# Sliding-window attention and a mixture of experts: one value load split, some work reordered, fillers added

## The chip, the cores and the metric

The kernel runs on one core of a Trainium2 chip. A core has a matrix engine (PE in the profile), a vector engine (DVE), a scalar engine (ACT), a general engine (POOL) and a sync engine (SP) that here only issues transfers. Each engine works through its own queue in order, and engines wait for one another by semaphores. Sixteen DMA engines move data between main memory and on-chip memory; transfers issued by POOL and by SP go through queues of their own, q0 and q1 in the profile. Matrix products land in PSUM, a small accumulator memory that DVE and ACT read. The metric is the device time of one execution in microseconds (us).

## What is computed

Attention over 8 batches of 8 heads, 576 positions, head size 64, in which a position sees itself and the 63 before it; its output is the input of a mixture of experts with one expert per batch:

```python
scores = scale * np.matmul(q, k.transpose(0, 1, 3, 2))
mask = (rel >= 0) & (rel < window)                 # window = 64
attn = softmax(np.where(mask, scores, -1e9))
x = np.matmul(attn, v)        # heads side by side: [8, 576, 512]
e_idx = np.argmax(x.mean(axis=1) @ w_gate, axis=1) # one of 8 experts per batch
h = np.maximum(x[b] @ w1[e_idx[b]], 0.0)           # w1: [8, 512, 1024]
out[b] = gate_w[b] * (h @ w2[e_idx[b]])            # w2: [8, 1024, 512]
```

Only the chosen expert of a batch is loaded. Which one it is, is known only when that batch's whole attention is done.

## The kernel before

**Units.** The work on attention is cut into 16 units: unit `t` is half of the heads of batch `t // 2`. A unit's q and k (`load_qk`, on POOL's queue, cast to bf16 on the way) are transposed on PE (`transpose_qk`) and copied out of PSUM by ACT or DVE (`leave_qk`). Then come three groups of scores (`scores(t, c)`, c = 0, 1, 2): small matmuls, an exp on ACT (line 389), and a multiplication by a 0/1 mask on DVE (line 396, `mask_out`). Units 0 and 1 do without the multiplication: there `add_outside` puts large negative numbers into PSUM with two matmuls per group, before the scores are added.

**Values.** `values(t, s)` multiplies the probabilities by v (line 417) and normalises on DVE (lines 431 and 433). v of a batch comes as one fp32 transfer on SP's queue (`load_v`, 36 blocks of 64 columns for 128 partitions). `cast_part` makes two fp16 copies of a unit's half of it: the whole tile (`va`), and two shifted halves, `low` and `high` (`vb`). Three fp32 v buffers are used in turn. The transfer is held back by a one-element write of POOL into the tile, and that write may read something that has to be there first (`behind`).

**Gate and experts.** After a batch's second unit, `transpose_x` turns x round, ACT also sums it, DVE multiplies the sums with the gate's weights, `gate` picks the expert and POOL loads its number into a register; `load_w1` and `load_w2` then fetch the two weight matrices (1 MB each in fp16). `expert_up` (line 561, eight per batch) makes h with ReLU on ACT (line 565), `expert_down` (line 575, and line 584 for the last 64 positions) makes the output, which DVE or ACT copies into one of six `ob` buffers, and SP sends it off (lines 579 and 592), five copies per batch.

**The order** is written out by hand, and each engine keeps it (`P` is `tc.keep_in_program_order`). A prologue handles units 0 to 3 and batch 0's gate line by line. Then a loop over `t` from 4 on mixes a unit of attention with pieces of the experts of earlier batches: each `experts(pace)` call takes about one `expert_up` or `expert_down` from a stream. In even `t` the loop also runs `next_gate` for batch `t // 2 - 1`, which issues that batch's weights, v of batch `t // 2 + 2`, and q and k. Four PSUM buffers are shared by everything. `busy(n)` issues n matmuls of 128x512 on a constant tile; nothing reads what they give.

The lines the change touches: `load_v` at 219, `cast_part` at 305, `gate` at 490, `load_w1` at 530, `load_w2` at 542, `expert_up` at 549, `expert_down` at 567, the prologue, and the loop body.

Of the kernel before, what the change touches and what calls it, by code (L numbers as in the profile page):

```python
# [156 lines left out]
def kernel(  # L157
# [10 lines left out]
    nc = tc.nc  # L168
# [49 lines left out]

    def load_v(b, behind=None):
# [7 lines left out]
        P(nc.sync.dma_start(out=vn, in_=vv[b]))  # L227
        v_tiles[b] = vn

    HM = NM // 2  # L230
# [240 lines left out]
    w1c = moe_w1.rearrange("e (kb p) f -> e p kb f", p=128)  # L471
    w2e = moe_w2.rearrange("e (g p i) d -> e p g i d", p=128, i=4)

    gparts = {}
# [15 lines left out]
    def gate(b):  # L490
# [3 lines left out]

        glog = small.tile([128, E], FP32, tag="glog")
        P(nc.vector.tensor_copy(out=glog, in_=gl[:, 0, 0:E]))
        gmx = small.tile([128, 8], FP32, tag="gmx")
# [25 lines left out]

    NQ = 2

    def w1_parts():
        return weights[0][0].rearrange("p k f -> p (k f)").rearrange(
            "p (h k f) -> p h k f", h=NQ, k=KB)

    def load_w1(b):  # L530
        if b == 0:

            src = w1c[experts_of[b]].squeeze(0)
            for hf in range(NQ):
                P(nc.gpsimd.dma_start(out=w1_parts()[:, hf],
                                      in_=src[:, :, ts(hf, F // NQ)]))
# [12 lines left out]
    def expert_up(b, ft):  # L549
        if b == 0:  # L550
            w1t, cols = w1_parts()[:, ft // 4], slice(ft % 4, 512, 4)
        else:
            w1t, cols = weights[b][0], slice(512 * (ft // 4) + ft % 4, 512 * (ft // 4 + 1), 4)
# [15 lines left out]
    def expert_down(b, mt):  # L569
# [3 lines left out]
        if mt < 4:  # L573
            for fb in range(FB):
                P(nc.tensor.matmul(  # L575
                    out=pso[:, 0, :], lhsT=hT[:, fb, ts(mt, 128)],
                    rhs=w2t[:, fb, :], start=(fb == 0), stop=(fb == FB - 1)))
            copy_on(nc.scalar if mt == 1 else nc.vector, ob, pso[:, 0, :])
            P(nc.sync.dma_start(out=out[b, ts(mt, 128), :], in_=ob))
# [184 lines left out]
    for t in range(START + 1, NU + LAG):  # L764
# [3 lines left out]
        def next_gate():  # L768
# [106 lines left out]
```

## Time and profile before

| what | us |
|---|---|
| median of 3 runs | 226.37 (226.18 to 226.79) |
| profiled execution | 226.16 |
| its span, first to last instruction | 224.1 |
| PE busy | 201.5 |
| DVE busy | 129.5 |
| ACT busy | 134.2 |
| POOL busy | 37.9 |

The table's lower part is from the first part of the profile's page. The second part cuts the span into forty slices of 5.6 us. The timeline gives instructions of one engine in order, with the idle time before each and what ended it in brackets. The view of waits adds up such idle times by who waited for whom. The chain of work follows the last instruction back to what released it, step by step. The view of stretches gives the engines' busy time, the granted PE clock and the DMA engines' share for any stretch of time. Lines such as L561 are lines of the kernel file.

### The profile page before, as it was taken

What the parts mean: (1) busy time and instruction counts of PE and PEld (TensorE: products, weight loads), DVE (VectorE), ACT (ScalarE), POOL (GpSimd) and SP (SyncE); (2) the same over time, 40 slices, a digit from 0 to 9 for tenths busy, and PEclk for the clock granted to TensorE, in tenths of its full rate; (3) what the DMA queues carried; (4) which work ended last, traced back from release to release, by engine and by line L of the source; (5) the groups of instructions that cost most, each with busy time, mean ns of one, the idle gap of its engine ahead of it and who ended that gap; (6) DMA issues with size and microseconds to landing.
All of it is one profiled execution on the core that took longest, in us unless ns stands there. A gap on an engine that the chain in (4) does not pass through costs nothing.

```text
span 224.1 us, 6989 instructions
## 1 busy us (share of the span) xinstructions
PE 201.5 (90%) x3011; PEld 141.9 (63%) x3012; DVE 129.5 (58%) x310; ACT 134.2 (60%) x220; POOL 37.9 (17%) x67
## 2 busy tenths in 40 slices
PE   7569779998799999989999998999999998999970
PEld 2247757755487568865686656875787557659630
DVE  2449695576856969284755667395939472420130
ACT  2176785963669656873869374967496557416400
POOL 7080360061000700052001600050002000200000
PEclk9988799999999999999999999999999999999996
DMA  5999999999999999999999999989955991399132
GB/s 70 239 253 244 159 188 218 245 251 226 231 233 249 252 214 240 235 283 207 246 229 300 169 236 228 271 203 221 243 155 87 212 256 40 56 225 255 68 140 69
DMA packets 29910, 45.64 MB, mean 204 GB/s; under 512 B 2480, under 2 KB 21936, under 8 KB 29872
## 3 DMA queue, kind: packets, MB, share of 16 engines
q0 software_dynamic: 13840, 26.22, 65.2%
q1 hardware_dynamic: 15232, 18.88, 27.5%
q8 instruction: 25, 0.41, 0.7%
q10 hardware_dynamic: 800, 0.03, 0.2%
q14 instruction: 13, 0.11, 0.1%
HBM read 61.90 MB, written 9.44 MB: 318 GB/s over the span
## 4 chain that ended last, share of the span: by engine, by line
PE 61%; DMA 13%; DVE 11%; ACT 8%; issue 3%; POOL 1%; POOLq 0%
PE php L561 24%; PE pso L575 19%; DMA w1t<-in_moe_w_dram 8%; ACT xT L462 5%; PE tp L334 5%; DMA kn<-in_k_dram 4%; PE op L417 4%; PE pso L584 3%; ACT hT L565 2%; DVE pt L396 2%; PE sp L374 2%; DVE vb L303 2%; DVE x L433 2%; PE tp L454 2%; PE gl L492 1%
## 5 line engine op out<-in xcount | busy, mean ns | idle before, releaser
L561 PE MATMUL php<-xT,w1t 128*128 128x288 f16 x512 | 70.0, 287 | 2.1 <-DMA w1t<-in_moe_w_dram 2.1
L565 ACT ACTIVATE hT<-php,gatew 128x576 f16<-128x576 f32 x64 | 47.1, 743 | 28.7 <-PE php L561 28.6
L561 PEld LDWEIGHTS <-w1t 128*128 128x128 f16 x512 | 56.0, 115 | 8.6 <-DMA w1t<-in_moe_w_dram 2.4
L575 PE MATMUL pso<-w2t,hT 128*128 128x512 f16 x256 | 60.2, 380 | 0.0
L389 ACT ACTIVATE pt<-sp 128x768 f16<-128x768 f32 x48 | 36.3, 815 | 9.3 <-PE sp L374 9.3
L575 PEld LDWEIGHTS <-hT 128*128 128x128 f16 x256 | 23.1, 98 | 25.8 <-issue 1.2
L303 DVE COPY ob<-pso 128x512 f32<-128x512 f32 x24 | 16.5, 688 | 24.4 <-PE pso L575 24.3
L538 POOL DMA_DIRECT2D w1t<-in_moe_w_dram x7 | 5.1, 730 | 136.7 <-DVE pt L396 91.9
L433 DVE TENSOR_TENSOR x<-op,linv 128x640 f16<-128x640 f32 x32 | 26.4, 825 | 1.1
L347 ACT COPY dst<-tp 128x1152 bf16<-128x1152 bf16 x16 | 17.9, 1120 | 14.0 <-PE tp L334 13.7
L396 DVE TENSOR_TENSOR pt<-pt,masks 128x768 f16<-128x768 f16 x42 | 22.8, 555 | 4.6 <-ACT pt L389 3.4
L462 ACT ACTIVATE xT<-tp 128x576 f16<-128x576 f16 x28 | 17.9, 646 | 6.3 <-PE tp L454 6.2
L417 PE MATMUL op<-vb,pt 128*64 128x65 f16 x320 | 17.0, 196 | 2.9 <-DVE pt L396 2.1
L417 PEld LDWEIGHTS <-pt 128*64 128x64 f16 x640 | 14.2, 111 | 5.7 <-DVE pt L396 2.5
L417 PE MATMUL op<-va,pt 128*64 128x65 f16 x320 | 16.7, 196 | 0.0
L303 DVE COPY vb<-va 64x1152 f16<-64x1152 f16 (+1 forms) x32 | 16.1, 504 | 0.7
L374 PE MATMUL sp<-dst 64*64 64x128 bf16 (+1 forms) x672 | 14.3, 218 | 1.6 <-ACT dst L301 0.8
L374 PEld LDWEIGHTS <-dst 64*64 64x64 bf16 x672 | 10.3, 110 | 8.5 <-issue 4.9
L484 DVE SCALAR_TENSOR_TENSOR gpart<-wg,pooled,gpart 128x8 f32<-128x8 f32 x21 | 4.8, 227 | 18.5 <-ACT xT L462 18.4
L431 DVE RECIPROCAL linv<-op 128x10 f32<-128x10 f32 x32 | 6.9, 216 | 13.7 <-PE op L417 13.6
L334 PE MATMUL tp<-ident,kn 128*64 128x128 bf16 x288 | 11.3, 225 | 2.9 <-DMA kn<-in_k_dram 2.9
L303 DVE CAST va<-vn 128x1152 f16<-128x1152 f32 x16 | 12.1, 758 | 3.2 <-DMA vn<-in_v_dram 3.1
(71 smaller groups left out, 178.6 us busy)
## 6 DMA issues: line engine op xcount, KB each, us to landing
w2t<-in_moe_w_dram POOLq DMA_DIRECT2D x8, 1024.0 KB, 17.3
out_dram<-ob SPq DMA_DIRECT2D x32, 256.0 KB, 6.8
w1t<-in_moe_w_dram POOLq DMA_DIRECT2D x7, 1024.0 KB, 9.1
qn<-in_q_dram POOLq DMA_DIRECT2D x16, 288.0 KB, 11.8
kn<-in_k_dram POOLq DMA_DIRECT2D x16, 288.0 KB, 12.8
w1t<-in_moe_w_dram POOLq DMA_DIRECT2D x2, 512.0 KB, 6.5
out_dram<-ob SPq DMA_DIRECT2D x16, 64.0 KB, 6.8
vn<-in_v_dram SPq DMA_DIRECT2D x8, 0.2 KB, 19.5
```

The costliest lines, as they stand in the source:

```text
L303: P(eng.tensor_copy(out=out, in_=in_))
L334: P(nc.tensor.transpose(out=tp[64 * s:64 * s + 64, ts(t, 128)], in_=src[:, s, ts(t, D)], identity=ident, tile_position=(0, 64 * s)))
L347: P(nc.scalar.copy(out=dst.rearrange("p (x r t) -> p x r t", x=2, t=NT), in_=view))
L374: P(nc.tensor.matmul(out=sp[64 * half:64 * half + 64, s, 64 * (qblk - 6 * c):64 * (qblk - 6 * c) + n], lhsT=kT[64 * s:64 * s + 64, ts(kblk ...
L389: P(nc.scalar.activation(out=pt, in_=sp[:, :, 0:384], func=AF.Exp, scale=scale))
L396: P(nc.vector.tensor_tensor(out=pt, in0=pt, in1=masks[:, c].rearrange("p s g w -> p s (g w)"), op=ALU.mult))
L417: P(nc.tensor.matmul(out=op[64 * half:64 * half + 64, xx, 65 * jj:65 * jj + 65], lhsT=pt[:, s, 64 * (g % 6):64 * (g % 6) + 64], rhs=win, s ...
L433: P(nc.vector.tensor_tensor(out=x[:, :, h0 * D:(h0 + 2) * D].rearrange("p j (x c) -> p x j c", x=2), in0=view[:, :, :, 0:64], in1=li[:, :, ...
L462: P(nc.scalar.activation(out=xT[:, kb, :], in_=tp[:, kl, 0:S], func=AF.Copy, accum_out=pooled[:, b, kb:kb + 1]))
L561: P(nc.tensor.matmul(out=php[:, sc, 0:288], lhsT=w1t[:, kb, cols], rhs=xT[:, kb, ts(sc, 288)], start=(kb == 0), stop=(kb == KB - 1)))
L565: P(nc.scalar.activation(out=hT[:, ft].rearrange("p (sc s) -> p sc s", sc=2), in_=php[:, :, 0:288], func=AF.Relu, scale=gatew[:, b:b + 1]))
L575: P(nc.tensor.matmul(out=pso[:, 0, :], lhsT=hT[:, fb, ts(mt, 128)], rhs=w2t[:, fb, :], start=(fb == 0), stop=(fb == FB - 1)))
```

## The change

It does eight things:

1. v of batch 3 comes in two transfers: blocks 0 to 19 where the whole transfer was issued before; the other 16 in the first pass of the loop, after the issue of batch 1's w1 and w2. The second is held by a POOL copy that reads a word of that w1.
2. Batch 0's w1 comes in three transfers of 256, 256 and 512 columns instead of two of 512; batch 0's w2 is read in runs of two rows instead of four, to fit. v of batch 2, held until the first half of w1 was there, is now held until the second of the three parts is there.
3. Batch 0's gate reads the logits out of PSUM and not from a copy.
4. In the prologue, two of unit 1's three `add_outside` move ahead of the transposes of its k, with two fillers; unit 1's whole-tile cast goes to ACT.
5. Fillers: `busy(1)` becomes `busy(3)` after unit 2's k, and `busy(2)` stands before batch 0's gate.
6. In the loop, from unit 6 on, the shifted halves of the next unit's v are cast after the third group of scores and its mask, not before.
7. The last output tile (batch 7, mt = 3) leaves PSUM in two halves, one by DVE and one by ACT, and goes out in two transfers, on SP's and on ACT's queue.
8. In even passes the gate's weight is also computed ahead of those shifted halves.

```diff
+    def load_rest(b, part, behind):
+        vn = v_tiles[b]
+        P(nc.gpsimd.tensor_copy(out=vn[:, part, 0:1], in_=behind))
+        P(nc.sync.dma_start(out=vn[:, part:NM, :], in_=vv[b][:, part:NM, :]))
...
+        if b:
+            glog = small.tile([128, E], FP32, tag="glog")
+            P(nc.vector.tensor_copy(out=glog, in_=gl[:, 0, 0:E]))
+        else:
+            glog = gl[:, 0, 0:E]
...
-    NQ = 2
+    PARTS = ((0, 256), (256, 256), (512, 512))
...
+            for i, (lo, n) in enumerate(PARTS):
+                P(nc.gpsimd.dma_start(out=w1_part(i), in_=src[:, :, lo:lo + n]))
...
-            out=weights[b][1].rearrange("p (g i) d -> p g i d", i=4),
-            in_=w2e[experts_of[b]].squeeze(0)))
+            out=weights[b][1].rearrange("p (g i) d -> p g i d", i=4 if b else 2),
+            in_=(w2e if b else w2f)[experts_of[b]].squeeze(0)))
...
+            if b == B - 1 and mt == 3:
+                oc = opool.tile([128, Dm], FP32, tag="ob", name="oc")
+                P(nc.vector.tensor_copy(out=ob[:, 0:256], in_=pso[:, 0, 0:256]))
+                P(nc.scalar.copy(out=oc[:, 0:256], in_=pso[:, 0, 256:512]))
+                P(nc.sync.dma_start(out=out[b, ts(mt, 128), 0:256], in_=ob[:, 0:256]))
+                P(nc.scalar.dma_start(out=out[b, ts(mt, 128), 256:512], in_=oc[:, 0:256]))
+                return
...
     transpose_qk(1, 0)
+    add_outside(1, 0)
+    add_outside(1, 1)
+    busy(2)
     transpose_qk(1, 1, leave=False)
     leave_qk(1, 1, A)
     load_qk(3)
     load_qk(4)
     cast_v(0)
-    cast_v(1)
-    for c in range(3):
-        add_outside(1, c)
+    cast_part(1, "whole", A)
+    cast_part(1, "low")
+    cast_part(1, "high")
+    add_outside(1, 2)
...
-    busy(1)
+    busy(3)
     pool_mm(1)
     pool_parts()
+    busy(2)
     gate(0)
...
-    load_v(2, w1_parts()[:, 0, 0, 0:1])
+    load_v(2, w1_part(1)[:, 0, 0:1])
     load_qk(6)
-    load_v(3)
+    load_v(3, part=20)
...
             load_w2(b)
+            if t == START + 1:
+                load_rest(3, 20, weights[b][0][:, 0, 0:1])
             if t // 2 + 2 < B:
                 load_v(t // 2 + 2)
...
             if gated:
                 cast_part(t + 1, "whole")
-            cast_part(t + 1, "low")
-            cast_part(t + 1, "high")
         experts(pace)
         if on:
             scores(t, 2)
         if gated and on:
             gate_weight(t // 2 - 1)
+        if ahead and t > 5:
+            cast_part(t + 1, "low")
+            cast_part(t + 1, "high")
```

More of the change, by code (lines that the diff above doesn't have):

```diff
@@ L217, with load_v @@
     v_tiles = {}
-    def load_v(b, behind=None):
+    def load_v(b, behind=None, part=0):
         vn = vpool.tile([128, NM, D], FP32, tag="vn")
@@ L226, in load_v @@
             P(nc.gpsimd.tensor_copy(out=vn[:, 0, 0:1], in_=behind))
-        P(nc.sync.dma_start(out=vn, in_=vv[b]))
         v_tiles[b] = vn
+        if part:
+            P(nc.sync.dma_start(out=vn[:, 0:part, :], in_=vv[b][:, 0:part, :]))
+        else:
+            P(nc.sync.dma_start(out=vn, in_=vv[b]))
+    def load_rest(b, part, behind):
+        vn = v_tiles[b]
+        P(nc.gpsimd.tensor_copy(out=vn[:, part, 0:1], in_=behind))
+        P(nc.sync.dma_start(out=vn[:, part:NM, :], in_=vv[b][:, part:NM, :]))
     HM = NM // 2
@@ L472 @@
     w2e = moe_w2.rearrange("e (g p i) d -> e p g i d", p=128, i=4)
+    w2f = moe_w2.rearrange("e (g p i) d -> e p g i d", p=128, i=2)
     gparts = {}
@@ L493, in gate @@
                            start=True, stop=True))
-        glog = small.tile([128, E], FP32, tag="glog")
-        P(nc.vector.tensor_copy(out=glog, in_=gl[:, 0, 0:E]))
+        if b:
+            glog = small.tile([128, E], FP32, tag="glog")
+            P(nc.vector.tensor_copy(out=glog, in_=gl[:, 0, 0:E]))
+        else:
+            glog = gl[:, 0, 0:E]
         gmx = small.tile([128, 8], FP32, tag="gmx")
@@ L522, with w1_part @@
     experts_of = {}
-    NQ = 2
-    def w1_parts():
-        return weights[0][0].rearrange("p k f -> p (k f)").rearrange(
-            "p (h k f) -> p h k f", h=NQ, k=KB)
+    PARTS = ((0, 256), (256, 256), (512, 512))
+    def w1_part(i):
+        lo, n = PARTS[i]
+        return weights[0][0].rearrange("p k f -> p (k f)")[
+            :, KB * lo:KB * (lo + n)].rearrange("p (k f) -> p k f", k=KB)
     def load_w1(b):
@@ L533, in load_w1 @@
             src = w1c[experts_of[b]].squeeze(0)
-            for hf in range(NQ):
-                P(nc.gpsimd.dma_start(out=w1_parts()[:, hf],
-                                      in_=src[:, :, ts(hf, F // NQ)]))
+            for i, (lo, n) in enumerate(PARTS):
+                P(nc.gpsimd.dma_start(out=w1_part(i), in_=src[:, :, lo:lo + n]))
         else:
@@ L550, in expert_up @@
         if b == 0:
-            w1t, cols = w1_parts()[:, ft // 4], slice(ft % 4, 512, 4)
+            part = min(ft // 2, 2)
+            at = 256 * (ft // 2) - PARTS[part][0]
+            w1t, cols = w1_part(part), slice(at + ft % 2, at + 256, 2)
         else:
```

## The prediction

> **What bounds the kernel.** I read the page's busy shares and forty slices first, then TensorE's (PE's) idle times in order of time, then the stretches that end in those idle times, then the DMA queues there. From the page:
>
> ```profile
> span 224.1 us, 6989 instructions
> ...
> PE 201.5 (90%) x3011; PEld 141.9 (63%) x3012; DVE 129.5 (58%) x310; ACT 134.2 (60%) x220; POOL 37.9 (17%) x67
> ...
> DMA  5999999999999999999999999989955991399132
> ```
>
> PE is busy 90% of the span, and from the second slice on the DMA engines are full too, up to about 160 us. So two limits lie close together: what shortens PE's waits helps only as long as the data then come. PE's idle times, from the timeline of PE (start, duration, in brackets the idle time before and what ended it):
>
> ```profile
> 14.30 0.69 PE L334 MATMUL tp<-ident,kn 128*64 128x128 bf16 x18 [1.61 <-DMA kn<-in_k_dram]
> ...
> 22.83 0.28 PE L675 MATMUL pool<-once,x 128*128 128x1 f16 x5 [0.49 <-DVE x L433]
> 23.72 0.36 PE L492 MATMUL gl<-gpart,onesf 128*128 128x8 f32 x2 [0.61 <-DVE gpart L686]
> ```
> ```profile
> 50.79 0.19 PE L417 MATMUL op<-vb,pt 128*64 128x65 f16 x1 [0.40 <-DVE vb L303]
> ...
> 60.06 1.17 PE L561 MATMUL php<-xT,w1t 128*128 128x288 f16 x8 [1.63 <-DMA w1t<-in_moe_w_dram]
> ```
> ```profile
> PE op L417 <- DVE pt L396: 2.1, 4, 1.1
> ...
> PE op L417 <- DVE vb L303: 0.8, 2, 0.4
> ```
>
> The last fence is the view of PE's waits (total, times, longest): four waits, 2.1 us, before the values' matmuls are ended by a mask (pt L396), all after 61 us, and there little else is left for PE to win. Before it the largest wait is the 1.63 us for batch 1's w1, at 60.06. What an earlier stage saves counts only as far as it arrives there.
>
> **The change, part by part.** (1) *Fourth v in two transfers.* Batch 1's w1 is asked for late and lands later. In the chain of work (start, duration):
>
> ```profile
> 26.19 5.47 DMA w1t<-in_moe_w_dram
> ...
> 46.75 13.26 DMA w1t<-in_moe_w_dram
> ```
>
> The DMA queues (packets, MB, share of 16 engines) from 48 to 52 us, then from 52 to 60, then the landing time of the w1 issued at 192 us:
>
> ```profile
> q1 hardware_dynamic: 910, 0.92, 104.1%
> q0 software_dynamic: 52, 0.05, 7.7%
> ```
> ```profile
> q0 software_dynamic: 352, 1.38, 85.0%
> q1 hardware_dynamic: 429, 0.43, 22.2%
> ```
> ```profile
> DMA to landing us min/median/max: 7.9/7.9/7.9
> ```
>
> The last is w1 of batch 7, issued with nothing else in flight: 7.9 us, against 13.26 here. From 48 to 52 us the SP queue (q1, v in small packets) moves 0.92 MB and POOL's queue (q0, weights, q and k) 0.05, though w1 was issued at 46.75; from 52 to 60 q1 still moves 0.43 MB beside it. v of batch 3 is 4608 runs of 256 B, 1.18 MB; the change leaves 16 of 36 blocks, 0.52 MB, until w1 has landed. That is the 0.43 MB and 0.09 of the flood. Beside q1, q0 ran 1.38 MB in 8 us; without it I give it the rate of q0 alone under (2), 0.90 MB in 4.5 us, so w1's 1.05 MB take 5.2 instead of 6.1 us, and the flood (0.92 MB in 4 us) ends 0.4 us sooner: w1 lands at 58.7 instead of 60.0. Bounds: 60.0, if the order of q0 alone sets it; 46.75 + 7.9 = 54.7, if nothing is in the way. PE stands ready at 60.06 - 1.63 = 58.43. I take 60.06 - 58.7 = 1.4 us, since the row of 52 to 60 prices it nearest; ends 0 and, if PE is also ready sooner, 2.5.
>
> The Trainium skill, "DMA: Bandwidth & Descriptors", section "Queues, rings and completion order", says that each DMA engine takes turns between queue rows packet by packet. By that, q1's small packets would have taken turns with w1's large ones from 48 on; the two rows of 48 to 52 do not show it (52 packets against 910), the rows after 52 do (352 against 429). By the rule alone w1 would gain only the 0.9 us of its share, and the sum below would be 2.3 instead of 2.8 us.
>
> What waits instead: the rest of v is held on POOL by a copy that reads w1, so POOL stands until w1 lands, with v of batch 4 and q, k of units 7 and 8 behind it; SP stands too, with v of batch 4 and the first outputs behind. The rows are, in turn: the output issued between 52.1 and 52.3 us (the last number is its landing time), ACT's seventh copy of an output, the first php of batch 2, and the landing time of the w1 issued between 74.4 and 74.6.
>
> ```profile
> out_dram<-ob SPq DMA_DIRECT2D x1, 256.0 KB, 22.5
> ```
> ```profile
> 76.50 0.59 ACT L301 COPY ob<-pso 128x512 f32<-128x512 f32 x1 [0.72 <-PE pso L575]
> ```
> ```profile
> 84.10 1.14 PE L561 MATMUL php<-xT,w1t 128*128 128x288 f16 x8
> ```
> ```profile
> DMA to landing us min/median/max: 9.1/9.1/9.1
> ```
>
> q and k lie behind w2 in q0 anyway, so their later issue costs nothing. The first output lands at 52.2 + 22.5 = 74.7; there are six ob buffers, five outputs a batch, so the seventh copy (76.50, on ACT) needs it: 1.8 us of room. PE coming 1.4 us sooner uses most of it up. Batch 2's w1 lands at 74.5 + 9.1 = 83.6 and is used at 84.1: 0.5 us of room, with more of v and outputs now beside it. I charge 0.6 us for the two together, ends 0 and 2 (as much as w1 of batch 1 loses now).
>
> (2) *w1 of batch 0 in three, w2 in shorter runs.* One more issue on POOL. Packets become 512 and 2048 B. The two halves' issue on POOL, and q0 from 28.5 to 33 us, where it runs alone with w1's halves:
>
> ```profile
> 26.19 1.50 POOL L535 DMA_DIRECT2D w1t<-in_moe_w_dram  x2 [10.09 <-DVE gatew L520]
> ```
> ```profile
> q0 software_dynamic: 893, 0.90, 122.3%
> ```
>
> Packet time, q0: 122.3% of 16 engines in 4.5 us over 893 packets of about 1024 B is 0.099 us; 85.0% of 16 in 8 us over 352 of mostly 4096 B is 0.309. On that line a 512 B packet is 0.064. The first quarter (512 packets) then flows in 2.1 us, the old half in 3.2: it comes 1.1 us sooner (PE's wait there is 0.46, below), but the first half needs 4.1, 1.0 later, and w2 (2048 B, 0.17) 0.4 more. So q0 gets 1.4 us more work, beside a POOL issue of 1.50/2 = 0.75.
>
> (3) *Gate without its copy, casts of unit 1 shared, masks added early.* Timelines of DVE, ACT, PE, DVE again, and the landing time of the v issued between 31.9 and 32.1 us:
>
> ```profile
> 15.20 0.76 DVE L303 CAST va<-vn 128x1152 f16<-128x1152 f32 x1 [3.09 <-DMA vn<-in_v_dram]
> ...
> 17.76 0.92 DVE L303 COPY vb<-va 64x1152 f16<-64x1152 f16 x2
> ...
> 24.12 0.17 DVE L496 COPY glog<-gl 128x8 f32<-128x8 f32 x1 [0.54 <-PE gl L492]
> ```
> ```profile
> 15.04 1.12 ACT L301 COPY dst<-tp 128x1152 bf16<-128x1152 bf16 x1 [0.24 <-PE tp L334]
> 17.55 2.21 ACT L389 ACTIVATE pt<-sp 128x768 f16<-128x768 f32 x3 [1.39 <-PE sp L374]
> ```
> ```profile
> 31.71 0.56 PE L561 MATMUL php<-xT,w1t 128*128 128x288 f16 x3 [0.46 <-DMA w1t<-in_moe_w_dram]
> ```
> ```profile
> 49.45 0.79 DVE L303 CAST va<-vn 128x1152 f16<-128x1152 f32 x1
> ```
> ```profile
> DMA to landing us min/median/max: 17.4/17.4/17.4
> ```
>
> DVE casts without a break from 15.20 to 18.68, then norms follow back to back. With unit 1's whole tile on ACT behind the k copy (15.04 + 1.12 = 16.16; a copy of as many elements, so another 1.12) the two halves run 17.3 to 18.25: 0.45 us sooner. ACT's three exps start near 17.3 instead of 17.55, as four of six mask matmuls move into PE's 1.61 us wait. The gate drops 0.17 + 0.03 us. So w1 of batch 0 goes out 0.6 us sooner and PE is up to 1.1 us ahead at 31.71 (both 0.46 and the earlier scores). None of it passes 49.45: the cast of unit 4 starts as v of batch 2 lands (32.0 + 17.4 = 49.4), and PE waits for that cast at 50.79. That v starts behind the first half of w1, which comes 1.0 - 0.6 us later. I take 0 for all of this at 51 us (ends 0.9 us lost and 0.9 won).
>
> (4) *Fillers.* Six more 128x512 matmuls in the waits of 1.61, 0.49 and 0.61 us. They hold the clock. Stretches of 3.41 us, with each engine's busy time; the column before the last two is the granted clock:
>
> ```profile
> 11.57:14.98 3.41, 1.66 (x61) 1.27 (x52) 0.54 (x4) 3.23 (x4) 3.29 (x5) 1.00 1.11 242
> 14.98:18.39 3.41, 3.41 (x62) 1.99 (x62) 3.05 (x6) 1.96 (x3) 1.13 (x2) 0.50 1.13 254
> ...
> 21.80:25.22 3.42, 2.18 (x63) 1.66 (x60) 2.13 (x10) 1.85 (x3) 0.00 (x0) 1.00 1.20 219
> 25.22:28.63 3.41, 3.41 (x50) 3.21 (x48) 2.81 (x7) 3.12 (x8) 2.44 (x4) 0.50 0.65 98
> ...
> 49.11:52.52 3.41, 2.58 (x57) 1.86 (x55) 2.74 (x7) 1.70 (x2) 2.00 (x3) 1.00 1.12 226
> ```
>
> 0.50 follows a stretch with 1.66 of 3.41 us busy, and one with 2.18, much of it very small matmuls; it does not follow the last row, 2.58. Filled, both should stay at 1.00. A filler is about 0.22 us at full clock, 0.4 at half; two fit before the gate's matmul (0.61). Cost 0 (0.4 us if the clock is half, hidden by the v of batch 2), gain inside (3).
>
> (5) *Shifted halves behind the third mask.* DVE in unit 6:
>
> ```profile
> 75.04 1.16 DVE L303 COPY vb<-va 64x1152 f16<-64x1152 f16 x2
> ```
>
> The two halves (1.16 us) stand ahead of the mask. Moved, the mask is done about 1.1 us sooner, as much as the longest of the four waits; of that one I leave 0.2, because an output copy stays ahead of the mask. DVE's sum is unchanged, so what follows starts when it did. 1.9 us, ends 0 and 2.1.
>
> (6) *Last output in halves.* DVE and SP at the end:
>
> ```profile
> 217.38 0.69 DVE L303 COPY ob<-pso 128x512 f32<-128x512 f32 x1 [1.40 <-PE pso L575]
> ```
> ```profile
> 216.01 2.10 SPq L592 DMA_DIRECT2D out_dram<-ob  x2
> 218.19 0.54 SPq L579 DMA_DIRECT2D out_dram<-ob  x1
> ```
>
> The copy of 0.69 us falls to about 0.4, but SP is busy to 218.11 with the two outputs before; only the ACT half leaves at 217.9. I take 0.1 us, ends 0.3 won and 0.3 lost (a second queue to close).
>
> Sum: 1.4 + 1.9 + 0 + 0.1 - 0.6 = 2.8 us. The profiled execution took 226.16 us, 2.1 over its span, so 223.4; it is 0.2 below the median of 226.37, so I forecast a median of **223.6**. Its own range, 222.3 to 224.7, is by the ends of (1): 1.1 more won there, with up to 0.2 in (5), or 1.1 less. Under 0.3% (0.7 us) a measurement can't tell from no change.
>
> **The rivals.** *The queue was the limit* (0.22): q0 gets 1.4 us more, w1 of batch 1 still lands near 60, or its gain goes at batch 2's w1. For it: DMA full from slice 3; against: q1's 0.43 MB really are out of the way. Left are (5) and (6): 226.4 - 2.0 = 224.4, and 225.4 with another 1 us lost later.
>
> *The clock falls at 52.5* (0.10). If PE is 1.0 us ahead and v of batch 2 is not, the stretch 49.11 to 52.52 keeps 2.58 - 1.0 = 1.6 us busy, less than the 1.66 after which 0.50 followed. The next stretch is full, 3.42 us, and half a clock adds 1.7: PE is ready for w1 at 58.43 + 1.7 = 60.1, (1) is gone, and 224.5 is left. The Trainium skill, "TensorE: Matmul & The Clock Gate", section "Part 1: The HAM clock gate", has the rate halve only after an idle window of about 3.4 us. By that rule nothing of the kind would happen and 223.6 stands; the trace has shown 0.50 after half-busy windows, so I keep the rival.
>
> *Slower: outputs held on SP* (0.12). SP has nothing to move from about 51 us, when the first part of v is through, until w1 lands near 58.7: 7.5 us. If that isn't made up, the first output lands at 74.7 + d, with d up to 7.5, and ACT's copy, then wanted at 76.5 - 1.4 = 75.1, waits d - 0.4, with a PSUM buffer held. It decides from d = 4.5 on (3.4 won without the 0.6, plus 0.7); at d = 5.5 the time is 226.4 - 3.4 + 5.1 = 228.1. For it: DMA full everywhere; against: q0 runs faster meanwhile, so most of it is made up.
>
> The remaining 0.06 is for parts that cancel to within 0.3%. Forecast 0.50. Faster: 0.50 + 0.21 + 0.09 = 0.80; same 0.07; slower 0.13. The range 221.8 to 226.0 takes in both middle rivals and the gain at w1's far end, and leaves out the slower case.
>
> **What would show it.** Right: no idle before batch 1's first php (60.06), or under 0.4 us; no idle ended by pt L396 before 65-column matmuls; granted clock 1.00 from 5 us to the end; PE still waiting near 51 us for vb, and longer than 0.8. Wrong: w1 of batch 1 landing at 60 again, idle before php near 82, an output copy on ACT near 75 that waits for a DMA, or a 0.50 after 49.

## The result and the profile after

The changed kernel takes 229.86 us (median of 4 runs, 228.49 to 230.84) where the kernel before takes 226.58 beside it (226.18 to 226.87): a ratio of 1.0147, 95% interval 1.0117 to 1.0178, so 3.3 us slower. The forecast was 223.6, with 226.0 as the upper end: the sign is wrong. Ratios and intervals leave out the runs that took over 1.5% longer than the fastest of the same kernel, medians take in all runs, so for a kernel with two groups of times the two can differ.

The profiled execution took 229.3 us, 1.7 over its span. From its page:

```profile
span 227.6 us, 7012 instructions
...
PE 202.0 (89%) x3018; PEld 140.1 (62%) x3018; DVE 127.8 (56%) x308; ACT 135.0 (59%) x222; POOL 39.4 (17%) x69
...
PEclk9999999999999979999999999999999999999997
...
DMA packets 34310, 45.64 MB, mean 201 GB/s; under 512 B 7136, under 2 KB 26208, under 8 KB 34272
```

The prologue keeps its full clock (9 from the first slice on; before, slices 3 to 5 had 8, 8 and 7). A 7 now stands in slice 15, that is after 80 us, where there was none. And 7136 packets are smaller than 512 B, where the kernel before had 2480. PE's idle times, from its timeline, then what PE waited for between 40 and 120 us (total, times, longest):

```profile
50.99 0.19 PE L425 MATMUL op<-vb,pt 128*64 128x65 f16 x1 [1.25 <-DVE vb L311]
...
59.13 1.14 PE L577 MATMUL php<-xT,w1t 128*128 128x288 f16 x8 [0.66 <-DVE ob L311]
...
81.78 1.17 PE L342 MATMUL tp<-ident,qn 128*64 128x128 bf16 x18 [4.47 <-ACT ob L309]
```
```profile
PE tp L342 <- ACT ob L309: 4.5, 1, 4.5
PE op L425 <- DVE vb L311: 1.5, 2, 1.3
```

The php of batch 1 starts at 59.13 instead of 60.06, and no mask (now line 404) ends a wait any more. What is new is one wait of 4.47 us before the transposes of unit 7's q. PE waits there for ACT, whose copy of an output (line 309) stood for 6.33 us. ACT's row, then the chain of work (start, duration), then SP's queue:

```profile
81.15 0.59 ACT L309 COPY ob<-pso 128x512 f32<-128x512 f32 x1 [6.33 <-DMA out_dram<-ob]
```
```profile
66.95 14.12 DMA out_dram<-ob
```
```profile
34.62 10.61 SPq L229 DMA_DIRECT2D vn<-in_v_dram  x1
57.95 0.94 SPq L236 DMA_DIRECT2D vn<-in_v_dram  x1
59.11 7.79 SPq L231 DMA_DIRECT2D vn<-in_v_dram  x1
66.95 7.95 SPq L603 DMA_DIRECT2D out_dram<-ob  x2
```

The copy needs the buffer of the first output. That one is issued at 66.95, behind the held second part of the fourth v (57.95) and v of batch 4 (59.11), and lands 14.12 us later, at 81.07; before it landed at 74.7. The idle time fills a whole stretch, and the next one runs at half clock (the first column behind the time is its length, then the busy times of PE, PEld, DVE, ACT and POOL; the last three columns are the granted clock, the DMA share and GB/s):

```profile
78.24:81.65 3.41, 0.00 (x0) 0.00 (x0) 0.00 (x0) 0.50 (x2) 0.00 (x0) 1.00 1.05 235
81.65:85.07 3.42, 3.29 (x42) 2.19 (x42) 1.38 (x3) 2.22 (x3) 0.00 (x0) 0.50 1.13 258
```

Why v and what stands behind it are late is in the queues (packets, MB, share of 16 engines), from 52 to 60 us as in the prediction, and in the landing time of the first part, issued at 34.62 (the last number):

```profile
q0 software_dynamic: 403, 1.59, 97.6%
q1 hardware_dynamic: 379, 0.10, 9.1%
```
```profile
vn<-in_v_dram SPq DMA_DIRECT2D x1, 640.0 KB, 29.4
```

q0 and q1 send about as many packets as each other, 403 and 379, but q1 moves 0.10 MB with them: 256 B each. Before, 429 packets moved 0.43 MB there, about 1 KB each. The parts of a divided v move in packets of 256 B, the whole v in packets four times as large. So the first part, which the prediction had through near 51 us, lands at 64.0: 20 blocks are no sooner through than all 36 were before (landed at 62.95), and 16 blocks, v of batch 4 and the outputs still stand behind them.

The last microseconds of the first output's delay have to do with batch 2's w1. Before, it was issued at 74.48, when that output was all but landed (74.67); now it is issued at 73.49, with the output still on its way. From 77 to 81 us the two queues send about as many packets as each other, and those of w1 are of 4 KB:

```profile
q0 software_dynamic: 164, 0.67, 84.2%
q1 hardware_dynamic: 157, 0.29, 21.8%
```

### The profile page after: what moved, and what is told of

Read it like the earlier page. It is cut to its first block, busy times and chain, and to the rows that moved or that the text cites. A ratio compares the mean times of both kernels' runs of the same rounds, so it can differ in the third digit from the quotient of the medians.

```text
span 227.6 us, 7012 instructions
## 1 busy us (share of the span) xinstructions
PE 202.0 (89%) x3018; PEld 140.1 (62%) x3018; DVE 127.8 (56%) x308; ACT 135.0 (59%) x222; POOL 39.4 (17%) x69
## 2 busy tenths in 40 slices
DMA packets 34310, 45.64 MB, mean 201 GB/s; under 512 B 7136, under 2 KB 26208, under 8 KB 34272
## 4 chain that ended last, share of the span: by engine, by line
PE 59%; DMA 17%; ACT 10%; DVE 6%; issue 3%; POOL 2%; POOLq 0%; SPq 0%; DVEq 0%; ACTq 0%
PE php L577 21%; PE pso L591 20%; DMA vn<-in_v_dram 7%; PE tp L342 6%; DMA out_dram<-ob 6%; PE op L425 4%; ACT pt L397 3%; DMA kn<-in_k_dram 3%; ACT xT L470 3%; ACT hT L581 3%; PE sp L382 2%; PE pso L608 2%; DVE vb L311 2%; PE tp L462 1%; DVE ob L311 1%
## 5 line engine op out<-in xcount | busy, mean ns | idle before, releaser
L591 PE MATMUL pso<-w2t,hT 128*128 128x512 f16 x256 | 61.0, 383 | 0.2
L577 PEld LDWEIGHTS <-w1t 128*128 128x128 f16 x512 | 55.1, 113 | 8.1 <-issue 0.6
L311 DVE COPY ob<-pso 128x512 f32<-128x512 f32 x23 | 15.9, 690 | 23.3 <-PE pso L591 23.2
L425 PE MATMUL op<-vb,pt 128*64 128x65 f16 x320 | 16.3, 196 | 2.1 <-DVE vb L311 1.5
L382 PE MATMUL sp<-dst 64*64 64x128 bf16 (+1 forms) x672 | 13.8, 213 | 3.2 <-ACT dst L309 2.0
L425 PE MATMUL op<-va,pt 128*64 128x65 f16 x320 | 16.0, 197 | 0.0
L309 ACT COPY ob<-pso 128x512 f32<-128x512 f32 x8 | 4.7, 586 | 18.7 <-PE pso L591 12.3
L342 PE MATMUL tp<-ident,qn 128*64 128x128 bf16 x288 | 11.5, 227 | 4.7 <-ACT ob L309 4.5
L342 PEld LDWEIGHTS <-qn 128*64 128x64 bf16 x288 | 9.2, 113 | 8.7 <-issue 7.7
```

The costliest lines, as they stand in the source:

```text
L311: P(eng.tensor_copy(out=out, in_=in_))
L342: P(nc.tensor.transpose(out=tp[64 * s:64 * s + 64, ts(t, 128)], in_=src[:, s, ts(t, D)], identity=ident, tile_position=(0, 64 * s)))
L382: P(nc.tensor.matmul(out=sp[64 * half:64 * half + 64, s, 64 * (qblk - 6 * c):64 * (qblk - 6 * c) + n], lhsT=kT[64 * s:64 * s + 64, ts(kblk ...
L425: P(nc.tensor.matmul(out=op[64 * half:64 * half + 64, xx, 65 * jj:65 * jj + 65], lhsT=pt[:, s, 64 * (g % 6):64 * (g % 6) + 64], rhs=win, s ...
L577: P(nc.tensor.matmul(out=php[:, sc, 0:288], lhsT=w1t[:, kb, cols], rhs=xT[:, kb, ts(sc, 288)], start=(kb == 0), stop=(kb == KB - 1)))
L591: P(nc.tensor.matmul(out=pso[:, 0, :], lhsT=hT[:, fb, ts(mt, 128)], rhs=w2t[:, fb, :], start=(fb == 0), stop=(fb == FB - 1)))
```

## Experiments

Theory A: the divided v moves in small packets, gets a small share beside the weights, comes late and makes the outputs behind it late. Theory B: it is the holding of the second part behind w1, whatever its packets. Theory C: other parts of the change cost the time. Unless said otherwise the diffs are against the changed kernel.

### The divided v: whole, alone, unheld, in large packets

Fourth v in one transfer:

```diff
-    load_v(3, part=20)
+    load_v(3)
...
-            if t == START + 1:
-                load_rest(3, 20, weights[b][0][:, 0, 0:1])
```

> The changed kernel with batch 3's v in one transfer again, everything else as changed. Theory A (the split v moves in small packets, so v of batches 3 and 4 and with them the first output come late, and the seventh output copy on ACT waits for its buffer): that wait, 6.3 us on ACT and 4.5 us on PE, is gone, and so are the half-clock stretch after it and its 1.7 us; 229.3 - 4.5 - 1.7 plus about 1 us of waiting for batch 1's w1 again: 223 to 225 us. Theory B (holding the second part behind w1 does it, whatever the packets): the same, 223 to 225. Theory C (the other parts, fillers, w1 in three and the last output, make it slower): 227 or more.

Measured: 224.66 us (223.25 to 228.0, 10 runs), ratio 0.9897 (0.9857 to 0.9937). Against 1.0147 that is 5.7 us: more than the whole loss comes from the divided v.

The same edit put into the kernel before, alone (diff against the kernel before; the changed `load_v` and the new `load_rest` are left out here):

```diff
...
-    load_v(3)
+    load_v(3, part=20)
...
+            if t == START + 1:
+                load_rest(3, 20, weights[b][0][:, 0, 0:1])
```

> The kernel before with only v of batch 3 in two transfers, the second held behind batch 1's w1. A and B: the first output lands at 80 us or later instead of 74.7, ACT's seventh output copy waits 4 to 6 us, PE 3 to 5 and a half-clock stretch follows; 226.4 + 4 to 6 = 230 to 232.5 us. C: 225 to 227, and batch 1's w1 a little sooner.

Measured: 228.37 us (226.21 to 229.96, 10 runs), ratio 1.0056 (1.0016 to 1.0095), 1.3 us slower: less than the 230 us that A and B had expected, more than the 227 of C. The same edit costs less there, and q1 from 48 to 52 us and the first part's landing time point to why:

```profile
q1 hardware_dynamic: 2613, 0.70, 88.7%
```
```profile
vn<-in_v_dram SPq DMA_DIRECT2D x1, 640.0 KB, 20.9
```

Here q1 sends 2613 packets, 0.70 MB, and the part lands at 55.1. In the changed kernel q0 has more to send in these 4 us (307 packets against 152), and batch 1's w1 is asked for 1.0 us sooner (46.10 instead of 47.13). There q1 gets through

```profile
q1 hardware_dynamic: 1468, 0.40, 47.5%
```

so over a third of the part's 0.66 MB is left, and goes on at q1's 0.10 MB in 8 us. By these rows the price of the small packets depends on how many of them meet the 4 KB packets of the weights. What it still costs here comes later: the second part lands at 71.0, and the ninth copy of an output waits for a buffer, with PE idle for 2.1 us.

```profile
83.10 0.69 DVE L311 COPY ob<-pso 128x512 f32<-128x512 f32 x1 [3.14 <-DMA out_dram<-ob]
```

The second part not held, but issued right behind the first:

```diff
     load_v(3, part=20)
+    load_rest(3, 20, None)
...
-        P(nc.gpsimd.tensor_copy(out=vn[:, part, 0:1], in_=behind))
+        P(nc.gpsimd.memset(vn[:, part, 0:1], 0.0))
...
-                load_rest(3, 20, weights[b][0][:, 0, 0:1])
+                pass
```

> The changed kernel with the second part of batch 3's v issued right behind the first, held by nothing, so that only the cut in two is left. A (small packets alone are enough): beside w1 of batch 1 and w2 the split v still gets under 20 KB per us; v of batch 4 lands at 75 us or later, the first output at 79 or later, and ACT waits 4 us or more; 228 to 231 us. B (the holding does it): the first output lands near 75, ACT waits under 1.5 us, 223 to 225 us. C: 228 or more without that wait.

Measured: 228.67 us (225.65 to 233.02, 10 runs), ratio 1.0022 (0.9975 to 1.0069). Nothing is held, and by the ratios it is still 2.8 us slower than the undivided v: the small packets cost that without any holding. The first part lands at 71.3, v of batch 4 at 78.6, the first output at 79.4. DVE waits for the first part, and ACT's seventh copy for the output, less than the 4 us that A had expected:

```profile
71.40 0.76 DVE L311 CAST va<-vn 128x1152 f16<-128x1152 f32 x1 [2.59 <-DMA vn<-in_v_dram]
```
```profile
79.43 0.59 ACT L309 COPY ob<-pso 128x512 f32<-128x512 f32 x1 [2.04 <-DMA out_dram<-ob]
```

Held, but with a first part of 32 blocks, which moves in 1 KB packets like the whole:

```diff
-    load_v(3, part=20)
+    load_v(3, part=32)
...
-                load_rest(3, 20, weights[b][0][:, 0, 0:1])
+                load_rest(3, 32, weights[b][0][:, 0, 0:1])
```

> Changed kernel with the first part of the fourth v of 32 blocks of 36 instead of 20; the second part (4 blocks, 131 KB) is held behind the second w1 as before. The first part then moves in 1024 B packets like the undivided v. Small packets (theory A): first part through near 67, the fifth v near 75 to 76, first output landed by 76, no output copy waits for a buffer, idle of 4.5 before the transpose of q7 gone, 224.2 to 225.8 (as with the undivided v, 224.7). Holding a part behind w1 as such (theory B): the fifth v stays past 76.5 and the first output past 79, 227.5 or more.

Measured: 224.44 us (223.2 to 227.72, 6 runs), ratio 0.9861 (0.9801 to 0.9921), as with the undivided v; the first part landed at 66.5, v of batch 4 at 76.2, the first output at 76.8. Its queues from 52 to 60 us:

```profile
q0 software_dynamic: 371, 1.45, 89.3%
q1 hardware_dynamic: 371, 0.38, 17.0%
```

371 packets against 371, and q1 moves 0.38 MB with its own; the fastest kernel below, with the whole v, has 368 against 369 there. The four kernels make a square, as ratios to the kernel before: small packets held 1.0147 (1.0096 when measured again, below) and not held 1.0022, large packets held 0.9861 and not held 0.9897. Not held, the two differ in the packets and in one more issue alone, and the intervals lie apart: theory A stands. B falls as the whole cause: with large packets the holding costs nothing. What it adds to small packets, 1.7 to 2.8 us by these ratios, isn't settled, since one of the two intervals (1.0059 to 1.0133) overlaps that of the kernel without the hold (0.9975 to 1.0069). Nor is the square a full one: with large packets only 4 blocks were held, and a larger rest in large packets wasn't tried.

The Trainium skill, "DMA: Bandwidth & Descriptors", section "Queues, rings and completion order", says that each DMA engine takes turns between queue rows packet by packet. These rows agree: 371 to 371 with 1 KB packets against 4 KB, 403 to 379 with 256 B. The row of 52 packets that the prediction set against the rule moved 0.05 MB, about 1 KB each, so it was not w1 with its 4 KB packets yet. By that rule, with the packet size known, the first part's rate beside w1 would have come out in the prediction.

### Which wait it ends in

Eight output buffers instead of six:

```diff
-    opool = ctx.enter_context(tc.tile_pool(name="opool", bufs=6))
+    opool = ctx.enter_context(tc.tile_pool(name="opool", bufs=8))
```

> The changed kernel with eight output buffers instead of six, so that the seventh copy need not wait for the first output. A and B: no wait of ACT for an output transfer near 75 us, no idle of 4.5 us on PE, clock 1.00 throughout; 223 to 225 us. If instead late data (w1 of batch 2, v of batch 4) would have stopped PE anyway, PE waits for those near 82 us and the time stays over 226.5. C: 228 or more.

Measured: 226.38 us (223.57 to 229.58, 10 runs), ratio 0.9970 (0.9938 to 1.0003). The seventh copy doesn't wait any more, and 4.0 us come back by the ratios. But the undivided v had a ratio of 0.9897, 1.7 us less again, so this wait isn't all.

The changed kernel itself, again:

> The changed kernel itself, unedited, beside the next two and the kernel before on one chip. If its 229.9 belongs to the kernel: 228.5 to 231 and a ratio of 1.010 to 1.018 again, with the first output landed at 80 to 82 and the seventh output copy waiting 5 us or more for it. If that profile was one of several courses that the same kernel can take: a median under 228 and a first output before 78.

Measured: 228.35 us (226.96 to 233.86, 7 runs), ratio 1.0096 (1.0059 to 1.0133): slower again, but the expected rows did not come. In this profile the first output lands at 78.8, the seventh copy runs at 80.66 and waits for no buffer. PE waits elsewhere, for DVE, where a cast waits for the first part of v itself (by the counts of its semaphore in the trace, 15 of its 16 engines' shares are there by 63.6, the last at 70.8). DVE and PE:

```profile
70.91 0.76 DVE L311 CAST va<-vn 128x1152 f16<-128x1152 f32 x1 [3.36 <-DMA vn<-in_v_dram]
```
```profile
73.37 0.56 PE L501 MATMUL gl<-gpart,onesf 128*128 128x8 f32 x2 [2.74 <-DVE gpart L493]
```

So the same program takes more than one course. With eight buffers and the last output in one piece:

```diff
-    opool = ctx.enter_context(tc.tile_pool(name="opool", bufs=6))
+    opool = ctx.enter_context(tc.tile_pool(name="opool", bufs=8))
...
-            if b == B - 1 and mt == 3:
...
-                return
```

> Changed kernel with eight output buffers and the last output in one piece; the fourth v stays divided in small packets. If the seventh copy's wait for a buffer is all that the divided v costs: 222.7 to 224.2, as with the undivided v and the same two edits (223.2). If the small packets cost something else besides: 224.5 to 226.

Measured: 225.89 us (223.05 to 229.04, 12 runs), ratio 0.9937 (0.9903 to 0.9971): the second case. DVE in its profile:

```profile
82.13 0.69 DVE L311 COPY ob<-pso 128x512 f32<-128x512 f32 x1 [3.88 <-DMA out_dram<-ob]
```

The first output lands at 82.04 here, and now the ninth copy waits for it: two more buffers only move the wait by two copies. The same kernel with `bufs=12`:

> Changed kernel with twelve output buffers instead of six and the last output in one piece; the fourth v stays divided in small packets. If waits for an output buffer are all that the divided v costs: no output copy waits for a landing, 222.8 to 224.0 (223.2 with the undivided v). If late v itself costs too (values of batch 1 late, as where the first part lands near 71): some runs at 223 and others at 225 to 227, median 224.3 to 226.

Measured: 225.68 us (222.56 to 227.8, 12 runs), ratio 0.9909 (0.9870 to 0.9949), in two groups: four runs from 222.56 to 223.49, the next at 225.56. The profile, of the first group, has no copy that waits for a landing, though the first output lands at 83.75. Three more runs of the same kernel, each for its profile:

> Changed kernel with twelve output buffers and the last output in one piece, again, for its profile. If late v itself makes the group at 225.7: in a run of that group the first part of the fourth v lands at 70 or later, and TensorE waits 1.5 to 3 us near 73 for what follows its cast. If another wait makes it: that part lands by 69 and the idle time lies elsewhere.

> The same, a second look: landing at 70 or later with a wait near 73 in a run of 225 or more, landing by 69 and no such wait in a run near 223.

> The same, a third look: landing at 70 or later with a wait near 73 in a run of 225 or more, landing by 69 and no such wait in a run near 223.

Measured: 225.72, 225.4 and 224.87 us (one run each). The rows of PE with the longest wait near there, one fence for each:

```profile
73.34 0.36 PE L501 MATMUL gl<-gpart,onesf 128*128 128x8 f32 x2 [2.35 <-DVE gpart L493]
```
```profile
52.07 0.19 PE L425 MATMUL op<-vb,pt 128*64 128x65 f16 x1 [1.78 <-DVE vb L311]
```
```profile
85.24 0.43 PE L577 MATMUL php<-xT,w1t 128*128 128x288 f16 x2 [2.10 <-DMA w1t<-in_moe_w_dram]
```

The first is the late first part (landed 70.8), as expected. The second isn't: the part landed at 64.2, and after 1.78 us of idle at 52 the clock was 0.50 from 52.52 to 55.93. That wait, for v of batch 2, is there with the undivided v too (below). The third is batch 2's w1, which landed at 85.2; from 77 to 85 us it takes turns with outputs and v (436 packets to 433). So once no copy can wait, other waits take its place, and two of these three are for transfers: the late part itself, and a w1 beside the late outputs. With enough buffers the divided v still costs 0.9909 - 0.9832 (undivided, below), some 1.7 us, though the two intervals overlap a little.

### The other parts

The shifted halves behind the third mask, alone, in the kernel before (diff against it):

```diff
-            cast_part(t + 1, "low")
-            cast_part(t + 1, "high")
         experts(pace)
...
+        if ahead and t > 5:
+            cast_part(t + 1, "low")
+            cast_part(t + 1, "high")
```

> Kernel before with the shifted halves behind the third mask, alone. By the prediction's fifth step the idle of 2.1 that the third mask ended in steps 6, 8, 10 and 12 goes and 1.9 are won: 224.4 to 225.2. If that idle was slack and other waits take its place: 226.3 to 226.9.

Measured: 223.84 us (223.22 to 224.43, 4 runs), ratio 0.9860 (0.9799 to 0.9922): 3.2 us faster, 1.8 to 4.6. In its view of PE's waits no mask stands any more; the same line's other row, 0.8 before, is:

```profile
PE op L417 <- DVE vb L303: 1.2, 2, 0.7
```

The prologue alone, with w1 in three parts: no divided v, halves where they were, last output whole.

```diff
-    load_v(3, part=20)
+    load_v(3)
...
-            if t == START + 1:
-                load_rest(3, 20, weights[b][0][:, 0, 0:1])
...
-            if b == B - 1 and mt == 3:
...
-                return
...
+            cast_part(t + 1, "low")
+            cast_part(t + 1, "high")
         experts(pace)
...
-        if ahead and t > 5:
-            cast_part(t + 1, "low")
-            cast_part(t + 1, "high")
```

> Changed kernel without the divided v, without the moved halves and without the divided last output: w1 in three parts with w2 in shorter runs, the gate without its copy, casts and masks on the other engines, the fillers. By the prediction these are worth nothing together: 226.2 to 227.2, with full clock from 6 to 49 us. Theory C (these make the changed kernel slower): 227.5 or more. If the saved half-clock stretches reach the end: 225.6 or less.

Measured: 226.82 us (225.11 to 228.16, 10 runs), ratio 1.0004 (0.9965 to 1.0043): nothing, and theory C falls for these parts. Where their gain goes is in the stretches of 3.41 us near 51 (busy times in the order PE, PEld, DVE, ACT, POOL, then the clock):

```profile
49.11:52.52 3.41, 1.22 (x33) 1.08 (x32) 2.31 (x5) 1.14 (x2) 0.83 (x2) 0.96 1.11 245
52.52:55.93 3.41, 3.41 (x16) 1.39 (x12) 1.04 (x2) 0.00 (x0) 0.00 (x0) 0.54 1.07 231
```

PE is ready for batch 2's values sooner, v of batch 2 isn't (landed 49.5), PE is busy for 1.22 of 3.41 us, and the next stretch runs at about half clock.

### The fastest, six more fillers, and the last output

Undivided v, eight buffers, last output in one piece:

```diff
-    load_v(3, part=20)
+    load_v(3)
...
-            if t == START + 1:
-                load_rest(3, 20, weights[b][0][:, 0, 0:1])
...
-    opool = ctx.enter_context(tc.tile_pool(name="opool", bufs=6))
+    opool = ctx.enter_context(tc.tile_pool(name="opool", bufs=8))
...
-            if b == B - 1 and mt == 3:
...
-                return
```

> Changed kernel with the fourth v undivided, eight output buffers instead of six, and the last output in one piece. Theory A: with the undivided v no output copy waits, so the two more buffers bring nothing, and the last output in one piece takes back about 1.1 (last matmul to the end of the span 6.7 instead of 7.8): 223.0 to 224.2. If the divided last output costs nothing: 224.7 as before. If output buffers bind still: 222.5 or less.

Measured: 223.19 us (222.99 to 224.09, 4 runs), ratio 0.9832 (0.9775 to 0.9889): faster than both kernels. No copy waits for a landing in it. Then six fillers were added to it, ahead of batch 1's first values:

```diff
     experts(2.0)
+    busy(6)
     values(2, 0)
```

> Changed kernel with the fourth v undivided, eight output buffers, the last output in one piece, and six filler matmuls ahead of batch 1's first values, in the wait of 1.55 us near 50.7. If the half clock from 52.5 to 55.9 comes from that wait (prediction's second rival): granted clock 1.00 there and 221.2 to 222.3 (223.2 without the fillers, less up to 1.7). If the fillers only push the values back, or w1 of batch 1 ends the next wait anyway: 223.0 to 223.8.

Measured: 222.98 us (222.74 to 226.19, 6 runs), ratio 0.9857 (0.9827 to 0.9887), not told apart from the one without. The clock from 52.52 to 55.93 is 1.00, but not because the wait near 51 was filled. Batch 1's first values run at 34.7 us; those that wait near 51 are batch 2's (`values(t, 0)` with t = 4). So the fillers stand at 33 us. Their row and the row of that wait, then that wait in the kernel without them, then the stretch with the fillers:

```profile
33.32 1.46 PE L676 MATMUL idle<-spin 128*128 128x512 bf16 x5
...
51.79 0.19 PE L425 MATMUL op<-vb,pt 128*64 128x65 f16 x1 [0.50 <-DVE vb L311]
```
```profile
50.70 0.19 PE L425 MATMUL op<-vb,pt 128*64 128x65 f16 x1 [1.55 <-DVE vb L311]
```
```profile
49.11:52.52 3.41, 2.47 (x33) 1.25 (x32) 2.76 (x6) 2.58 (x5) 2.96 (x5) 1.00 1.13 255
```

PE comes to that wait 2.1 us later (51.79 - 0.50 instead of 50.70 - 1.55) and waits 0.50 instead of 1.55 us; the stretch holds 2.47 us of work instead of 1.59, and the clock stays. But batch 1's w1 is asked for later as well (47.65 instead of 45.51; 0.9 us of that were there before the fillers), and PE waits for it:

```profile
60.26 0.93 PE L577 MATMUL php<-xT,w1t 128*128 128x288 f16 x6 [0.83 <-DMA w1t<-in_moe_w_dram]
```

The divided last output put back into that kernel:

```diff
+            if b == B - 1 and mt == 3:
+                oc = opool.tile([128, Dm], FP32, tag="ob", name="oc")
+                P(nc.vector.tensor_copy(out=ob[:, 0:256], in_=pso[:, 0, 0:256]))
+                P(nc.scalar.copy(out=oc[:, 0:256], in_=pso[:, 0, 256:512]))
+                P(nc.sync.dma_start(out=out[b, ts(mt, 128), 0:256], in_=ob[:, 0:256]))
+                P(nc.scalar.dma_start(out=out[b, ts(mt, 128), 256:512], in_=oc[:, 0:256]))
+                return
```

> The fastest kernel so far (undivided v, eight output buffers, fillers near 51; 223.0) with the divided last output of the change put back. By the ends of the traces (6.4 to 7.0 us from the last matmul to the end of the span where it is whole, 7.8 to 8.5 where it is divided, 6.7 once): 223.7 to 224.4. By the prediction's sixth step: 222.7 to 223.3.

Measured: 224.86 us (222.95 to 230.7, 13 runs), ratio 0.9896 (0.9865 to 0.9927): 0.9 us more by the ratios, though the intervals overlap. Instead of that, the last output whole but on ACT's queue:

```diff
-            P(nc.sync.dma_start(out=out[b, ts(mt, 128), :], in_=ob))
+            last = b == B - 1 and mt == 3
+            P((nc.scalar if last else nc.sync).dma_start(out=out[b, ts(mt, 128), :], in_=ob))
```

> The same kernel with the last output whole but issued on ACT's queue instead of SP's. If a second queue at the end is what costs 1 us: 223.7 to 224.3 and about 7.7 us from the last matmul to the end of the span. If the two copies one behind the other, and SP's issue of 0.54, make it: 222.6 to 223.1 and 6.5 or less.

Measured: 224.61 us (221.22 to 228.65, 7 runs), ratio 0.9840 (0.9788 to 0.9892): too wide to tell. Its trace tells a little: 7.9 us from the last matmul to the end of the span, as with the divided output. The end of the changed kernel, DVE, ACT and SP:

```profile
219.74 0.42 DVE L597 COPY ob<-pso 128x256 f32<-128x256 f32 x1 [1.40 <-PE pso L591]
```
```profile
220.20 0.37 ACT L598 COPY oc<-pso 128x256 f32<-128x256 f32 x1 [4.43 <-DVE ob L597]
220.60 0.39 ACTq L600 DMA_DIRECT2D out_dram<-oc  x1
```
```profile
220.61 0.54 SPq L599 DMA_DIRECT2D out_dram<-ob  x1
```

ACT's half starts when DVE's half is done (220.16), not beside it, and SP is busy with the two outputs before until 220.52, so the last issues stand 0.9 us behind the last matmul (219.71), as before (217.34 and 218.19). From the last issue to the end of the span it is then 7.0 us instead of 5.9. Over all profiles, from the last matmul to the end: 6.4 to 7.0 us (mean 6.7) in eleven with the whole output on SP's queue, 6.8 to 8.5 (mean 7.7) in seven with the divided one.

## Why the prediction was wrong

**(1) The fourth v in two transfers: wrong, and the step that failed is the size of its packets.** The prediction counted "4608 runs of 256 B" and, in the same part, quoted 910 packets for 0.92 MB, 1 KB each; it did not notice that the whole v is sent in joined runs, nor ask whether its parts would be. They aren't. From this follows the error in "SP has nothing to move from about 51 us, when the first part of v is through": it was through at 64.0. The term, 1.4 won less 0.6, became 1.3 lost alone and 4.5 to 5.7 lost with the rest (1.0096 or 1.0147 against 0.9897). The charge of 0.6 named the right wait, the seventh copy's need of the first output, and mis-sized its delay: the prediction saw 1.8 us of room there, and the copy stood for 6.33 us.

What was to be won there did come: alone in the kernel before, the division brought batch 1's w1 from 60.0 to 57.5, where 58.7 was forecast. But the prologue's edits, which ask for it sooner, do as much without it: it lands at 57.4 in the fastest kernel, with the whole v, and at 57.5 in the changed kernel, with both.

**The rival that came** is the slower one, outputs held on SP. It decided from a delay of 4.5 us; the delay was 6.4 (81.07 against 74.7). By its own formula that gives 226.4 - 3.4 + 6.0 = 229.0, against 229.3 in the profile. The sign that it named came too, an output copy on ACT that waits for a DMA. That the time comes so close is luck in part: of its 3.4 us won, (5) gave 3.2 instead of 1.9, and (6) lost 1.0. Its reason was the hold, and the square of four kernels has the packets first. It was also not one wait: a second profile of the same kernel has its longest wait between 40 and 120 us at 73, for the late v itself.

**(2) and (4) Packets and fillers of the prologue: the packet's price right, the fillers right in this profile.** 0.064 us were worked out for a packet of 512 B. In the changed kernel the queue's row from 28.5 to 30.5 us:

```profile
q0 software_dynamic: 568, 0.28, 116.1%
```

116.1% of 16 engines in 2 us over 568 packets of mostly 512 B is 0.065. The first quarter of w1 landed 4.96 us after its issue, where the first half had taken 5.47: 0.5 us sooner, not 1.1. The clock shows no half stretch before 80 us. That was luck in part: of the sixteen profiles with this prologue, seven have a stretch at half clock again before 23 us, such as the one with nothing held:

```profile
PEclk9976999999999999999999999999999999999996
```

**(3) The gate, casts and masks: right in the sum (0, measured 0.1), and the second rival is part of why.** In the three profiles with the new prologue, the whole v and no more fillers, the clock falls to 0.50, 0.54 and 0.55 near 52.5, as that rival had it. The fastest kernel without fillers:

```profile
49.11:52.52 3.41, 1.59 (x38) 1.21 (x35) 2.45 (x5) 1.16 (x2) 1.20 (x2) 0.95 1.11 244
52.52:55.93 3.41, 3.41 (x11) 1.04 (x8) 0.69 (x2) 0.00 (x0) 0.00 (x0) 0.55 1.06 229
```

1.59 of 3.41 us busy is followed by 0.55; the rival had asked for less than 1.66. In the changed kernel that stretch was busier, and the clock stayed:

```profile
49.11:52.52 3.41, 1.89 (x53) 1.67 (x54) 2.16 (x5) 1.71 (x2) 0.00 (x0) 1.00 1.19 241
52.52:55.93 3.41, 3.41 (x54) 1.85 (x51) 1.82 (x5) 0.60 (x1) 0.00 (x0) 1.00 1.07 210
```

The Trainium skill, "TensorE: Matmul & The Clock Gate", section "Part 1: The HAM clock gate", has the rate halve after an idle window of about 3.4 us; that it does so "only" then is the prediction's word. The changed kernel agrees at 78.24 to 81.65, where PE was busy 0.00 us. The fastest kernel differs at 49.11 to 52.52: PE was busy 1.59 us there, not idle, and the measurement decides.

**(5) The shifted halves: right in place, under-sized.** 1.9 us were forecast; alone it won 3.2 (1.8 to 4.6), and no mask ends a wait any more. The forecast lies within the interval. What is won beyond the 2.1 us of idle wasn't followed further.

**(6) The last output: wrong in sign.** Forecast 0.1 won with 0.3 lost as the worse end; the traces have some 1.0 lost (7.7 against 6.7 us on average). That the halves run one behind the other was missed; what was named (a second queue to close) was taken as too small. One trace with only ACT's queue used shows the same 7.9 us, which points to that queue; which step behind the issue takes the longer isn't settled.

**The sum.** With 3.2 won in (5), nothing in (2) to (4), 1.0 lost in (6) and 4.5 to 5.7 lost in (1), 2.3 to 3.5 us are lost; 2.2 and 3.3 were measured. The terms of (1) are differences to the undivided v, so what this tests is that kernel: 3.2 - 1.0 = 2.2 us won, and 2.3 measured.

## What to carry to other kernels

Before a transfer is cut, work out the packet size of the whole from the queue's row (bytes by packets) and ask what the parts will have: where two queues are full, each gets turns and not bytes, so a fourth of the packet size is a fourth of the rate. A transfer made late delays everything behind it on its queue, and more buffers only move the wait on, to the next copy and then to the next transfer. Where a program can end in several waits, a single profile names one of them; a second profile of the same kernel is worth a run. And before a wait is filled, find in the timeline which call of the program it stands at.

## What was not expected of the hardware

- The parts of v of 16 and 20 blocks go in 256 B packets, the whole of 36 and a part of 32 blocks in 1 KB packets, from the same rows in memory.
- Turns between two queues held to within 6% over 8 us (371 to 371 and 403 to 379 packets), with 1 KB and with 256 B against 4 KB, while both queues had work.
- The clock fell to about half after stretches in which PE was busy 1.2 to 1.6 of 3.41 us, with no idle time over 2 us in them (1.20, 1.22, 1.41 and 1.59 near 51 us in four profiles), and stayed after 1.89 in the changed kernel. These rows give no sharp line: they are cut at the same times for all profiles, while each clock steps at its own. With twelve buffers a row of 1.57 kept full clock; cut where that clock steps, 48.60 to 52.01, it is 1.83.
- One engine's share of a transfer can lag: 15 of 16 engines were through with the first part at 63.6 us, the last at 70.8 (in another profile at 64.8 and 70.8), while a queue of larger packets was running.
